# One chunk's second MLP in plain float32, its weight split moved to the next chunk's loads, and more masks on ScalarE

## The chip, the cores and the metric

The kernel runs on one core of a Trainium2 chip. The metric is the device time of one execution in microseconds (us), from launch to end; a lower time is better. The core has five engines that run their own instruction streams and wait for each other by semaphores: TensorE (PE; its weight loads are shown apart as PEld), VectorE (DVE), ScalarE (ACT), GpSimd (POOL) and SyncE (SP), which here only issues the DMAs.

## The reference

Three layers follow each other, all in float32: attention in which each query keeps its 32 best keys, and two MLPs over the 2304 rows (4 batches x 576 queries) of 512 features.

```python
scores = 0.125 * q @ k^T                  # 4 batches, 8 heads, 576 x 576, head size 64
kth    = 32nd largest of each row
attn   = softmax(where(scores >= kth, scores, -1e9));  x = attn @ v      # -> 2304 x 512
h = x @ w_in   (512 x 2048);   x = (h - tanh(h)) @ w_out                 # first MLP  (m = 0)
h = x @ w_in2  (512 x 2048);   x = where(h > 0, h, exp(min(h,0)) - 1) @ w_out2   # second MLP (m = 1)
```

## The kernel before, in words

The 2304 rows are cut into six chunks of 384 rows (`CHUNKS`; numbered 0 to 5 below, the "first chunk" is chunk 0). For each chunk the attention comes first and then the two MLPs; the MLPs of one chunk are woven into the attention of the next, so that TensorE has matmuls while VectorE looks for the 32 best keys.

**Attention.** A chunk has 4 head pairs and 8 groups of three 128-row tiles. A group takes four ticks of the hand-written order: in each tick `find` takes the eight largest of each tile (MAX8, L295) and, in the first three ticks, `drop` strikes them out (MATCH_REPLACE8, L309). In the fourth tick the rows are masked. VectorE does it with one instruction (L316), on exponentials that ScalarE made earlier (L299); or, for the first `MASK_ACT[chunk]` tiles of a group, ScalarE does it with a Prelu (L311) and an Exp that also sums (L312). `MASK_ACT` is 3 of 3 tiles in chunk 0, 1 of 3 in chunk 1, and 0 after that.

**MLPs.** An MLP has 16 steps (`ft`), 128 of the 2048 hidden features each. In a step `first` makes h from the 512 inputs (L435), ScalarE and VectorE apply the function (`gate`), and `second` adds the step's share to three PSUM banks (L471). Every product of float32 numbers is made from three products of "float32r" numbers: each operand is split into a rounded high part and a low rest (`split`, L114 to L116: ScalarE copies, GpSimd subtracts), and high x high, low weight x high and high weight x low are summed. So `first` has 12 matmuls of 384 columns a step and `second` 9 of 512 columns. The scores of chunk 0 (L270), attention x v (L355) and the small matmuls of the norm use plain float32, and the trace shows each of them as two instructions: L270 stands in the program 48 times and in the trace 96 times.

**Weights.** They come from outside as pairs of 32-bit words that are put together on the chip. `prepare` does this once for each of the 64 weight tiles of 128 x 512 (two MLPs, 16 steps, two halves), in chunk 0: a 512 KB load (`wr`), three ScalarE instructions (L144 to L146), one on VectorE (L147, `wf`), a GpSimd multiply (L150), then the split on ScalarE and GpSimd (`wp`, L152), and a store of high and low (512 KB) to a scratch in DRAM. Chunks 1 to 5 load high and low from it (L164, 512 KB). The eight pairs of tiles in `EARLY` (the first MLP's last four steps and the second MLP's first four) are prepared ahead, during chunk 0's attention, and chunk 0 loads them too. Weight tiles have 5 and 6 buffers, `wr` 3, `wf` 2; loads are issued 6 steps ahead.

**Order.** The order of the calls is written out by hand by ticks. From it a planner makes each engine's instruction order, by a simulated timeline, so an engine's order can differ from the program's where the plan sees a wait. All DMAs go through SyncE's queue in order. At the turn from the first to the second MLP, `between` copies the result (L485), transposes it (L488) and splits it into zh and zl (L490 on ScalarE, L491 on VectorE).

In the profile chunk 0's first MLP runs from about 188 to 286 us and its second from 290 to about 421 us, beside chunk 1's attention and the first groups of chunk 2's; chunk 1's second MLP and its weight loads, which are issued six steps earlier, follow between about 475 and 600 us. About the last 200 us hold chunk 5's MLPs alone.

Of the kernel before, what the change touches and what calls it, by code (L numbers as in the profile page):

```python
# [8 lines left out]
F32 = mybir.dt.float32  # L9
# [10 lines left out]
P = 128  # L20
# [25 lines left out]
MASK_ACT = [3, 1, 0, 0, 0, 0]  # L46
# [38 lines left out]
def tile_topk_attention_two_mlps(  # L85
# [35 lines left out]

    scratch = {
# [10 lines left out]
    def prepare(m, ft, half):  # L133

        raw = sb.tile([P, 512], I64, tag="wr", name=f"wr{m}_{ft}_{half}", bufs=RAW_BUFS)
        nc.sync.dma_start(raw, (w1, w2)[m][ft][:, half * 512 : half * 512 + 512])
        words = raw.bitcast(F32).rearrange("p (n w) -> p n w", w=2)  # L140
        sign = sb.tile([P, 512], BF16, tag="wsg", name=f"wsg{m}_{ft}_{half}", bufs=2)
        w = sb.tile([P, 512], F32, tag="wf", name=f"wf{m}_{ft}_{half}", bufs=2)
        low, scaled = words.bitcast(U32)[:, :, 0], words[:, :, 1]
        nc.scalar.activation(sign, words[:, :, 1], AF.Sign)  # L144
        nc.scalar.activation(scaled, words[:, :, 1], copy, scale=2.0**-112)  # L145
        nc.scalar.activation(low.bitcast(I32), low, copy, scale=2.0**-29 * (1 - 2.0**-20), bias=-0.5 + 7.5 * 2.0**-20)  # L146
        nc.vector.scalar_tensor_tensor(  # L147
            w.bitcast(U32), scaled.bitcast(U32), 3, low, op0=ALU.logical_shift_left, op1=ALU.bitwise_or
        )
        nc.gpsimd.tensor_mul(w, w, sign)  # L150
        wt = weight_tile(half, f"wp{m}_{ft}_{half}")
        split(wt[:, 0], wt[:, 1], w)  # L152
        nc.sync.dma_start(f(scratch[m, ft, half]), f(wt))
        return wt

    def load_next():
        if loads:
            ci, m, ft = loads.pop(0)
            for half in range(2):
                if ci == 0 and m * NF + ft not in EARLY:  # L160
                    weights[ci, m, ft, half] = prepare(m, ft, half)
                    continue
                wt = weights[ci, m, ft, half] = weight_tile(half, f"wt{ci}_{m}_{ft}_{half}")
                nc.sync.dma_start(f(wt), f(scratch[m, ft, half]))  # L164
# [261 lines left out]
    def first(ci, m, ft):  # L426
        n = SIZES[ci]
        xh, xl = x_tiles[ci] if m == 0 else z_tiles[ci]
        h = bank("h", f"h{ci}_{m}_{ft}", 2)[:, :n]
        wv = weights.pop((ci, m, ft, 0)).rearrange("p a (k c) -> p a k c", c=P)  # L430
        jobs = [(wi, xs, kt) for wi, xs in ((0, xh), (1, xh), (0, xl)) for kt in range(4)]
        late = (n // P - 1) * P
        for cs in (slice(0, late), slice(late, n)) if m == 1 and ft < PARTED and late else (slice(0, n),):
            for a, (wi, xs, kt) in enumerate(jobs):
                nc.tensor.matmul(h[:, cs], wv[:, wi, kt], xs[:, kt, cs], start=(a == 0), stop=(a == len(jobs) - 1))  # L435
# [8 lines left out]
    def gate(ci, m, ft):  # L444
        n = SIZES[ci]
        h, t = parts[ci, m, ft]
        g = sb.tile([P, NMAX], F32, tag="g", name=f"g{ci}_{m}_{ft}")[:, :n]
# [7 lines left out]
        gh = sb.tile([P, NMAX], F32R, tag="gh", name=f"gh{ci}_{m}_{ft}")[:, :n]  # L455
# [4 lines left out]
    def second(ci, m, ft):  # L460
# [5 lines left out]
        jobs = [(k, t) for k in range(3) for t in range(nt)]  # L466
        if ft == NF - 1:
            jobs.sort(key=lambda x: x[1])
        for k, t in jobs:
            gx, wi = ((gh, 0), (gh, 1), (gl, 0))[k]  # L470
            nc.tensor.matmul(  # L471
                acc[ci, m][:, t],
                gx[:, t * P : t * P + P],
                wt[:, wi],
                start=(ft == 0 and k == 0),
                stop=(ft == NF - 1 and k == 2),
            )

    def between(ci):

        a = acc.pop((ci, 0))
        z_tiles[ci] = zh, zl = tuple(sb.tile([P, NPAIR, NMAX], F32R, tag=f"x{c}", name=f"z{c}{ci}") for c in "hl")
        y = [sb.tile([P, 512], F32, tag="y", name=f"y{ci}_{t}", bufs=Y_BUFS) for t in range(SIZES[ci] // P)]
        for t in range(SIZES[ci] // P):
# [4 lines left out]
            cs = slice(t * P, t * P + P)  # L489
            nc.scalar.activation(zh[:, :, cs], pv, copy)  # L490
# [163 lines left out]
```

## Time and profile before

| | |
|---|---|
| time, median of 3 runs | 1289.49 us (1286.18 to 1289.66) |
| the profiled execution, its own time | 1289.64 us |
| its span, from the first to the last instruction | 1287.8 us |
| busy, share of the span: PE, PEld, DVE, ACT, POOL | 92%, 76%, 77%, 64%, 46% |
| granted TensorE clock, mean share of full speed | 0.963 |
| DMA, mean | 222 GB/s |

A busy PE is not a PE at its peak: matmuls overlap in the pipeline and their ends are modelled. For TensorE the spacing of matmuls in a long run says more than the mean duration of one. Idle time is charged to the last thing waited for.

### The profile page before, as it was taken

How to read it: one execution, taken by the hardware profiler on the slowest of the kernel's cores; microseconds unless marked ns; L12 is line 12 of the kernel's file. 1: busy time of each engine (PE TensorE's matmuls, PEld its weight loads, DVE VectorE, ACT ScalarE, POOL GpSimd, SP SyncE). 2: the span in 40 equal slices, each digit the busy share in tenths (PEclk: the TensorE clock that was granted, in tenths of full speed). 3: DMA queues.
4: the chain of work that ended last, by engine and by line, in shares of the span. 5: the costliest groups of instructions: out<-in, count | busy, mean ns of one | idle time of the engine just before them, and what ended most of it. 6: DMA issues, size and time to landing. Idle time of an engine off the chain costs nothing.

```text
span 1287.8 us, 19866 instructions
## 1 busy us (share of the span) xinstructions
PE 1189.0 (92%) x6424; PEld 981.9 (76%) x6424; DVE 993.4 (77%) x1950; ACT 819.2 (64%) x1780; POOL 592.4 (46%) x629
## 2 busy tenths in 40 slices
PE   4576889979989999999999999999999999999998
PEld 2333468758768888888877888988988978899896
DVE  7999999999899888789889789889888886100111
ACT  6999969898888445656556666566665545332333
POOL 4666559867886332434432344443334322233221
PEclk9976699989999999999999999999999999999999
DMA  7778446995778865667765668776677645677672
GB/s 249 241 254 263 152 145 225 326 285 170 243 234 316 286 218 167 213 221 251 222 204 178 208 226 270 234 222 197 222 214 235 208 150 182 210 252 257 215 246 76
DMA packets 97448, 286.14 MB, mean 222 GB/s; under 512 B 12096, under 2 KB 27968, under 8 KB 97344
## 3 DMA queue, kind: packets, MB, share of 16 engines
q1 hardware_dynamic: 97344, 284.87, 68.4%
q8 instruction: 51, 0.84, 0.3%
q14 instruction: 53, 0.43, 0.1%
HBM read 246.55 MB, written 38.27 MB: 221 GB/s over the span
## 4 chain that ended last, share of the span: by engine, by line
PE 68%; DVE 11%; ACT 10%; DMA 6%; issue 2%; POOL 2%; SPq 0%; POOLq 0%; ACTq 0%; DVEq 0%
PE h L435 28%; PE acc L471 26%; PE av L355 6%; DMA wr<-in_w_dram 5%; DVE vm L295 4%; PE pt L337 4%; DVE w L309 3%; PE ps L272 2%; PE ps L273 2%; DVE wf L147 2%; ACT wr L146 1%; ACT s L274 1%; ACT wr L145 1%; DMA kraw<-in_kT_dram 1%; ACT wp L115 1%
## 5 line engine op out<-in xcount | busy, mean ns | idle before, releaser
L116 POOL TENSOR_TENSOR gl<-g,gh 128x384 fp32r<-128x384 f32 x192 | 203.6, 1062 | 417.4 <-ACT gh L115 355.9
L295 DVE MAX8 vm<-w 128x8 f32<-128x576 f32 x432 | 321.0, 751 | 5.3
L471 PE MATMUL acc<-wt,gh 128*128 128x512 f32 x1008 | 271.6, 398 | 0.3 <-ACT gh L115 0.3
L309 DVE MATCH_REPLACE8 w<-vm,w 128x576 f32<-128x576 f32 x288 | 213.0, 740 | 0.0
L471 PEld LDWEIGHTS acc<-wt,gh 128*128 128x128 f32 x1008 | 184.7, 188 | 33.8 <-issue 1.2
L274 ACT ACTIVATE s<-ps 128x288 f32<-128x288 f32 (+1 forms) x320 | 125.5, 409 | 85.0 <-PE ps L273 78.8
L337 PE MATMUL pt<-ident,e 128*128 128x128 f32 (+1 forms) x720 | 120.1, 293 | 45.4 <-ACT e L312 25.9
L295 DVE MAX8 vm<-s 128x8 f32<-128x576 f32 x144 | 108.1, 750 | 64.9 <-ACT s L274 64.2
L435 PE MATMUL h<-zh,wt 128*128 128x384 f32 (+2 forms) x768 | 151.8, 329 | 5.5 <-ACT zh L490 3.9
L115 ACT ACTIVATE gh<-g 128x384 fp32r<-128x384 f32 x192 | 100.5, 525 | 87.5 <-DVE g L449 41.6
L471 PE MATMUL acc<-wt,gl 128*128 128x512 f32 x504 | 153.9, 401 | 0.8 <-POOL gl L116 0.8
L338 ACT ACTIVATE ph<-pt 128x384 f32<-128x384 f32 (+1 forms) x240 | 110.1, 490 | 53.5 <-PE pt L337 52.3
L337 PEld LDWEIGHTS pt<-ident,e 128*128 128x128 f32 (+1 forms) x720 | 89.8, 142 | 71.3 <-ACT e L312 28.7
L435 PE MATMUL h<-xh,wt 128*128 128x384 f32 x672 | 141.3, 340 | 1.6 <-DVE g L454 1.6
L435 PEld LDWEIGHTS h<-zh,wt 128*128 128x128 f32 x768 | 126.6, 193 | 17.0 <-ACT zh L490 5.3
L449 DVE SCALAR_TENSOR_TENSOR g<-t,h 128x384 f32<-128x384 f32 x96 | 52.2, 544 | 110.9 <-ACT t L441 110.6
L435 PEld LDWEIGHTS h<-xh,wt 128*128 128x128 f32 x672 | 117.4, 188 | 10.0 <-DVE g L454 1.8
L316 DVE SCALAR_TENSOR_TENSOR e<-s,vm,e 128x576 f32<-128x576 f32 x115 | 112.2, 981 | 2.6 <-ACT e L299 0.5
L471 PEld LDWEIGHTS acc<-wt,gl 128*128 128x128 f32 x504 | 92.3, 189 | 21.5 <-POOL gl L116 2.8
L355 PE MATMUL av<-ph,vraw 128*64 128x384 f32 (+3 forms) x640 | 106.1, 440 | 1.9 <-ACT s L274 1.9
L309 DVE MATCH_REPLACE8 w<-vm,s 128x576 f32<-128x576 f32 x144 | 106.6, 740 | 0.0
L116 POOL TENSOR_TENSOR wp<-wf,wp 128x512 fp32r<-128x512 f32 x64 | 87.5, 1368 | 29.8 <-ACT wp L115 29.1
(78 smaller groups left out, 2008.2 us busy)
## 6 DMA issues: line engine op xcount, KB each, us to landing
wt<-w SPq DMA_DIRECT2D x336, 512.0 KB, 4.3
wr<-in_w_dram SPq DMA_DIRECT2D x64, 512.0 KB, 4.7
w<-wp SPq DMA_DIRECT2D x64, 512.0 KB, 3.6
kraw<-in_kT_dram SPq DMA_DIRECT2D x120, 144.0 KB, 3.9
vraw<-in_vL_dram SPq DMA_DIRECT2D x64, 160.0 KB, 3.4
qraw<-in_qT_dram SPq DMA_DIRECT2D x88, 96.0 KB, 3.9
out_dram<-o SPq DMA_DIRECT2D x16, 256.0 KB, 6.3
out_dram<-o SPq DMA_DIRECT2D x4, 128.0 KB, 5.2
```

The source lines that it names most:

```text
L115: nc.scalar.activation(hi, src, copy)
L116: nc.gpsimd.tensor_sub(lo, src, f(hi))
L274: nc.scalar.activation(s[lo:hi, cs], pt[lo:hi, :HS], copy)
L295: nc.vector.max(g.vm[:, j, min(r, 1)], u.s[t] if r == 0 else g.w[j])
L309: nc.vector.match_replace(g.w[j], v, u.s[t] if r == 0 else g.w[j], FILL)
L316: nc.vector.scalar_tensor_tensor(u.e[t], u.s[t], v[:, 7:8], u.e[t], op0=ALU.is_ge, op1=ALU.mult, accum_out=g.sum[:, j : j + 1])
L337: nc.tensor.transpose(pt[:kn, j * P : j * P + P], v.e[t][:, k0 : k0 + kn], ident)
L338: nc.scalar.activation(g.ph[:kn, blk, :nq], pt[:kn, :nq], copy)
L355: nc.tensor.matmul(pt[h * D : h * D + D, :n], v.vraw[h][:kn, blk], v.g.ph[:kn, blk, cs], start=(blk == 0), stop=(blk == NB - 1),)
L435: nc.tensor.matmul(h[:, cs], wv[:, wi, kt], xs[:, kt, cs], start=(a == 0), stop=(a == len(jobs) - 1))
L449: nc.vector.scalar_tensor_tensor(g, t, -1.0, h, op0=ALU.add, op1=ALU.max)
L471: nc.tensor.matmul(acc[ci, m][:, t], gx[:, t * P : t * P + P], wt[:, wi], start=(ft == 0 and k == 0), stop=(ft == NF - 1 and k == 2),)
```

## The change

The second MLP of chunk 0, and only that one, takes plain float32 operands: one product instead of three, so 4 matmuls in `first` and 3 in `second` for each step in the program. Its weights are then not split in `prepare`: GpSimd's multiply writes the weight tile itself, and 256 KB go to a scratch of their own (`single`). zl, the split of the gate and gl are left out for it. When chunk 1 loads these 32 tiles it loads 256 KB, splits them (ScalarE and GpSimd) and stores the 512 KB that chunks 2 to 5 load. `MASK_ACT` of chunk 1 goes from 1 to 3. The diff, without the lines that only rename:

```diff
-MASK_ACT = [3, 1, 0, 0, 0, 0]
+MASK_ACT = [3, 3, 0, 0, 0, 0]
...
-        nc.gpsimd.tensor_mul(w, w, sign)
         wt = weight_tile(half, f"wp{m}_{ft}_{half}")
-        split(wt[:, 0], wt[:, 1], w)
-        nc.sync.dma_start(f(scratch[m, ft, half]), f(wt))
+        if m == 1:
+            nc.gpsimd.tensor_mul(f(wt[:, 0]), w, sign)
+            nc.sync.dma_start(single[m, ft, half], f(wt[:, 0]))
+        else:
+            nc.gpsimd.tensor_mul(w, w, sign)
+            split(wt[:, 0], wt[:, 1], w)
+            nc.sync.dma_start(f(scratch[m, ft, half]), f(wt))
...
+            if ci == 0 and m == 1:
+                nc.sync.dma_start(f(wt[:, 0]), single[m, ft, half])
+            elif ci == 1 and m == 1:
+                nc.sync.dma_start(f(wt[:, 1]), single[m, ft, half])
+                split(wt[:, 0], wt[:, 1], f(wt[:, 1]))
+                nc.sync.dma_start(f(scratch[m, ft, half]), f(wt))
+            else:
                 nc.sync.dma_start(f(wt), f(scratch[m, ft, half]))
...
+        plain = (ci, m) == (0, 1)
+        if plain:
+            jobs = [(f(wv[:, 0, kt]), f(xs[0][:, kt])) for kt in range(4)]
...
+        if (ci, m) == (0, 1):
+            parts[ci, m, ft] = gh, None
+            return
...
+        terms = ((f(gh), f(wt[:, 0])),) if (ci, m) == (0, 1) else ((gh, wt[:, 0]), (gh, wt[:, 1]), (gl, wt[:, 0]))
...
+            if ci == 0:
+                nc.scalar.activation(f(zh[:, :, cs]), pv, copy)
+                continue
             nc.scalar.activation(zh[:, :, cs], pv, copy)
             nc.vector.tensor_sub(zl[:, :, cs], pv, f(zh[:, :, cs]))
```

## Rows read from the trace of the kernel before

**Rows 1.** Busy time by engine in stretches (length; busy us; clock; DMA share, GB/s).

```profile
154.00:174.00 20.00, 17.02 (x79) 10.30 (x78) 18.11 (x39) 14.80 (x35) 6.78 (x11) 0.91 0.23 62
174.00:194.00 20.00, 17.56 (x87) 15.66 (x86) 20.00 (x42) 13.58 (x29) 15.21 (x14) 0.91 0.56 191
194.00:217.00 23.00, 21.83 (x123) 19.91 (x122) 23.00 (x43) 21.30 (x46) 22.57 (x25) 1.00 0.74 243
217.00:241.00 24.00, 22.91 (x151) 18.51 (x150) 23.93 (x45) 22.32 (x49) 22.40 (x22) 1.00 0.81 262
241.00:262.00 21.00, 19.32 (x111) 17.37 (x110) 20.73 (x44) 16.75 (x37) 13.51 (x16) 1.00 1.02 356
262.00:281.00 19.00, 14.73 (x107) 10.37 (x105) 19.00 (x36) 17.51 (x40) 15.18 (x16) 1.00 1.01 294
290.00:421.00 131.00, 122.28 (x720) 102.31 (x721) 124.86 (x240) 111.41 (x243) 100.09 (x92) 0.97 0.72 242
505.00:600.00 95.00, 95.00 (x520) 81.36 (x519) 81.06 (x163) 56.85 (x127) 35.50 (x39) 1.00 0.71 224
```

**Rows 2.** The chain that ended last, single pieces (start us, length us, what).

```profile
82.52 1.98 ACT e L311 x3
...
199.14 0.77 DVE e L316 x2
...
272.01 9.04 DMA kraw<-in_kT_dram
...
283.14 5.09 DMA wr<-in_w_dram
...
323.19 4.33 DMA wr<-in_w_dram
...
801.59 3.70 PE av L355 x40
...
1140.82 2.10 PE acc L471 x9
1142.92 2.08 PE h L435 x12
```

**Rows 3.** Instruction groups of the whole run (count; busy us, mean ns).

```profile
L116 POOL TENSOR_TENSOR gl<-g,gh 128x384 fp32r<-128x384 f32 x192 | 203.6, 1062 | 417.4 <-ACT gh L115 355.9 <-PE acc L471 38.2 <-PE ps L273 12.8
...
L316 DVE SCALAR_TENSOR_TENSOR e<-s,vm,e 128x576 f32<-128x576 f32 x115 | 112.2, 981 | 2.6 <-ACT e L299 0.5
...
L115 ACT ACTIVATE gh<-g 128x384 fp32r<-128x384 f32 x192 | 100.5, 525 | 87.5 <-DVE g L449 41.6 <-PE acc L471 16.2 <-DVE g L454 15.7
...
L116 POOL TENSOR_TENSOR wp<-wf,wp 128x512 fp32r<-128x512 f32 x64 | 87.5, 1368 | 29.8 <-ACT wp L115 29.1
...
L115 ACT ACTIVATE wp<-wf 128x512 fp32r<-128x512 f32 x64 | 40.6, 634 | 4.1 <-POOL wf L150 4.1
...
L312 ACT ACTIVATION_READ_ACCUMULATOR e<-e,b 128x1 f32 x29 | 6.0, 206 | 0.0
```

**Rows 4.** TensorE on line L435 in one stretch (matmuls, then weight loads).

```profile
290.00:421.00 131.00, 52.89 (x276) 46.76 (x276) 0.97 0.72 242
```

**Rows 5.** The same for line L471, in two stretches.

```profile
290.00:421.00 131.00, 41.60 (x153) 27.20 (x154) 0.97 0.72 242
505.00:600.00 95.00, 42.81 (x162) 29.60 (x162) 1.00 0.71 224
```

**Rows 6.** TensorE's timeline at 73 us (start, length of the run, what).

```profile
73.16 0.89 PE L270 MATMUL ps<-kraw,qraw 64*128 64x288 f32 x3
```

**Rows 7.** Line L270 (count; ns min/median/max, first and last start).

```profile
L270 PE MATMUL ps<-kraw,qraw x96: 402/685/847, 4.3 to 141.0; 64*128 64x288 f32 x96
```

**Rows 8.** DMA issues from 505 to 600 us (count, size, median us to landing).

```profile
wt<-w SPq DMA_DIRECT2D x34, 512.0 KB, 4.3
```

**Rows 9.** The same from 225 to 290 us.

```profile
wt<-w SPq DMA_DIRECT2D x16, 512.0 KB, 8.4
```

**Rows 10.** SyncE's waits over the whole run (us in total, times, longest).

```profile
SPq L139 <- DVE wf L147: 68.1, 40, 4.0
```

More of the change, by code (lines that the diff above doesn't have):

```diff
@@ L119, in bank @@
         return ps.tile([P, 512], F32, tag=tag, name=name, bufs=bufs)
+    single = {
+        (m, ft, half): dr.tile([P, 512], F32, tag=f"f{m}_{ft}_{half}", name=f"f{m}_{ft}_{half}")
+        for m in range(1, 2)
+        for ft in range(NF)
+        for half in range(2)
+    }
     scratch = {
@@ L149, in prepare @@
         )
-        nc.gpsimd.tensor_mul(w, w, sign)
         wt = weight_tile(half, f"wp{m}_{ft}_{half}")
-        split(wt[:, 0], wt[:, 1], w)
-        nc.sync.dma_start(f(scratch[m, ft, half]), f(wt))
+        if m == 1:
[5 more added lines that the diff above has]
+            nc.sync.dma_start(f(scratch[m, ft, half]), f(wt))
         return wt
     def load_next():
[L157 to L163, printed above, removed]
+        if not loads:
+            return
+        ci, m, ft = loads.pop(0)
+        for half in range(2):
+            if ci == 0 and m * NF + ft not in EARLY:
+                weights[ci, m, ft, half] = prepare(m, ft, half)
+                continue
+            wt = weights[ci, m, ft, half] = weight_tile(half, f"wt{ci}_{m}_{ft}_{half}")
+            if ci == 0 and m == 1:
[5 more added lines that the diff above has]
+            else:
                 nc.sync.dma_start(f(wt), f(scratch[m, ft, half]))
@@ L427, in first @@
         n = SIZES[ci]
-        xh, xl = x_tiles[ci] if m == 0 else z_tiles[ci]
+        xs = x_tiles[ci] if m == 0 else z_tiles[ci]
+        plain = (ci, m) == (0, 1)
         h = bank("h", f"h{ci}_{m}_{ft}", 2)[:, :n]
         wv = weights.pop((ci, m, ft, 0)).rearrange("p a (k c) -> p a k c", c=P)
-        jobs = [(wi, xs, kt) for wi, xs in ((0, xh), (1, xh), (0, xl)) for kt in range(4)]
+        if plain:
+            jobs = [(f(wv[:, 0, kt]), f(xs[0][:, kt])) for kt in range(4)]
+        else:
+            jobs = [(wv[:, wi, kt], x[:, kt]) for wi, x in ((0, xs[0]), (1, xs[0]), (0, xs[1])) for kt in range(4)]
         late = (n // P - 1) * P
         for cs in (slice(0, late), slice(late, n)) if m == 1 and ft < PARTED and late else (slice(0, n),):
-            for a, (wi, xs, kt) in enumerate(jobs):
-                nc.tensor.matmul(h[:, cs], wv[:, wi, kt], xs[:, kt, cs], start=(a == 0), stop=(a == len(jobs) - 1))
+            for a, (w, x) in enumerate(jobs):
+                nc.tensor.matmul(h[:, cs], w, x[:, cs], start=(a == 0), stop=(a == len(jobs) - 1))
         t = sb.tile([P, NMAX], F32, tag="t", name=f"t{ci}_{m}_{ft}")[:, :n]
@@ L465, in second @@
         gh, gl = parts.pop((ci, m, ft))
-        jobs = [(k, t) for k in range(3) for t in range(nt)]
+        terms = ((f(gh), f(wt[:, 0])),) if (ci, m) == (0, 1) else ((gh, wt[:, 0]), (gh, wt[:, 1]), (gl, wt[:, 0]))
+        jobs = [(k, t) for k in range(len(terms)) for t in range(nt)]
         if ft == NF - 1:
@@ L469, in second @@
         for k, t in jobs:
-            gx, wi = ((gh, 0), (gh, 1), (gl, 0))[k]
+            gx, w = terms[k]
             nc.tensor.matmul(
@@ L473, in second @@
                 gx[:, t * P : t * P + P],
-                wt[:, wi],
+                w,
                 start=(ft == 0 and k == 0),
-                stop=(ft == NF - 1 and k == 2),
+                stop=(ft == NF - 1 and k == len(terms) - 1),
             )
```

9 lines of the change are left out of this document (6 added, 3 removed).

## The prediction

> **What bounds the kernel now.** I read the busy time by stretches first, cut at the groups of chunk 1's attention [rows 1]. Up to 281 us VectorE is full (from 174 us on it idles 0.3 us in a stretch at most) while TensorE still has gaps. From 505 to 600 us it is the other way round: TensorE 95.00 of 95, VectorE 81.06. So what is saved on VectorE counts only before about 421 us, and whatever TensorE is given costs time as soon as its gaps are used up. ScalarE must be read beside VectorE: in 194 to 217, 217 to 241 and 262 to 281 us it idles only 1.70, 1.68 and 1.49 us; in the other three stretches 4.25 to 6.4 us.
>
> Then the chain of waits [rows 2]. Between 270 and 380 us it runs through the making of weights: DMAs of `wr` (5.09 and 4.33 us shown, two of some eight), each issued when VectorE's L147 has freed a raw buffer (SyncE waited 68.1 us for L147 in all [rows 10]), and one `kraw` DMA of 9.04 us at 272 us, where the 16 DMA engines were full (share 1.02 and 1.01 [rows 1]). Late in the run the chain is only `first` and `second`: 2.08 us for 12 matmuls, 2.10 us for 9 [rows 2], so a step costs TensorE 4.18 us.
>
> **Masks: 16 leave VectorE.** Chunk 1 has 8 groups, and two more tiles of each go to ScalarE. On VectorE each takes 0.77 us at best (the chain's piece with its sum read) and 0.98 us by the mean, 1.06 with the read [rows 2, 3]. On ScalarE each adds a Prelu at 0.66 us (three in 1.98 us [rows 2]) and a sum read of 0.1 to 0.21 us [rows 3]; the Exp was there before and only moves to the fourth tick. A group thus sheds 1.5 to 2.1 us of VectorE and gains 1.5 to 1.7 us of ScalarE. Six groups lie in the six stretches before 281 us. In three of them ScalarE's idle time is just what is added, so VectorE's gain is lost to ScalarE; in the other three it counts: 3 x 1.5 to 2.1 = 4.6 to 6.4 us. ScalarE's own waits for others don't all vanish, so I take **-4.0** (bounds 0 and -12.7, which is six full groups). Behind the later Exp the group's transposes wait; they come in the next tick or the one after, some 5 us on, and are covered while TensorE has step work.
>
> **Shorter making of weights, less traffic at the turn.** Of the 32 tiles of the second MLP 8 are prepared early, 24 in the stage. Each sheds a ScalarE copy (634 ns) and a GpSimd subtract (1368 ns) [rows 3], and 256 KB of store; the 8 early ones also come back as 256 KB. At the turn, around 241 to 281 us, those are 8 x 256 KB = 2.1 MB less in full DMA queues, at 294 to 356 GB/s some 6 us of transfer. Loads there landed after 8.4 us [rows 9], elsewhere 4.3 [rows 8], and behind the 5.09 us DMA at 283 us stands the ScalarE work on `wr`, with zh of the turn behind it. VectorE was full until 281 us, so only part reaches the end: **-1.5** (0 to -4.1, the difference of the two landings). The planner makes new orders here, so this is the softest term.
>
> **The second MLP of chunk 0, 290 to 421 us.** It sheds 16 gate splits on ScalarE (525 ns) and GpSimd (1062 ns) [rows 3], 24 weight splits as above, three zl on VectorE and the last four masks. ScalarE loses 16 x 0.525 + 24 x 0.634 = 23.6 us less 4 x 0.8, GpSimd 16 x 1.06 + 24 x 1.37 = 50 us: both fall far from full, and VectorE has at least 3 us more. TensorE becomes the question. A plain float32 matmul is two instructions; one of 128 rows by 128 columns of weights isn't in the trace, L270's 64 by 128 is nearest. Three of L270 at full clock took 0.89 us, the last of them 0.40 [rows 6, 7], so they start (0.89 - 0.40)/2 = 0.245 us apart for 288 columns, hence 0.326 for 384 and 0.435 for 512. `first` takes 8 x 0.326 = 2.61, `second` 6 x 0.435 = 2.61: 5.22 us a step in place of 4.18, +1.04. The first two steps are cut in 256 and 128 columns, where 12 + 12 float32r matmuls have no such advantage; I count nothing for their `first` and half for their `second`: 14 x 1.04 + 2 x 0.5 = **+15.6 us of TensorE's time**. Bounds: what those three rows leave, 0.245 to 0.297 (0.89/3), the upper one being +34 us; I stay at the lower, for the run's last matmul must end before it can be counted.
>
> Does it fit? In 290 to 421 us TensorE issues 720 matmuls [rows 1]: 276 of L435 and 153 of L471 [rows 4, 5]. L435 is 19 whole `first` and 2 cut ones (48 pieces, 2.7 us each `first`): 19 x 2.08 + 5.4 = 44.9; L471 17 x 2.10 = 35.7. The other 291 belong to attention. In 505 to 600 us the full TensorE ran 18 steps (162/9 [rows 5]) = 75.2 us, and the rest of 95 us went to attention: 155 others or a little more, 0.128 us each. At that price 291 cost 37.2, so the stretch holds 118 us of work, of 131; with the change 133, 2 us over. But 80 of the 291 are half-width attention x v, 40 in 3.70 us [rows 2], 0.0925 each: 2.8 us less, 130.6. So TensorE's gaps are just used up: between -3 and +4 I take **-0.5**. Here the change's VectorE gain is worth nothing.
>
> **A rule against it.** The row gives plain float32 a price of 5.22/4.18 = 1.25 of the split form. The Trainium skill, FP8 and Floating Point Precision, section TensorE Precision Notes, says that true float32 takes four passes through the array; against three products of one pass that would be a third more, 16 x 4.18/3 = 22.3 us in place of 15.6, by estimate, and the sum would be some 6.7 us worse. The trace agrees with the four (two instructions, each at half the column rate), but here a float32r matmul also costs more than its columns, which the rule leaves out; the row decides.
>
> **Chunk 1's second MLP, about 475 to 600 us.** It gains 32 loads of 256 KB in place of 512, 32 splits and 32 stores of 512 KB. ScalarE gets 32 x 0.634 = 20.3 us, GpSimd 32 x 1.368 = 43.8: over 95 us they go from 56.9 to 77 and from 35.5 to 79 [rows 1]. DMA gains 8.4 MB, 88 GB/s: 224 becomes 312, near the 294 to 356 at which loads landed after 8.4 us. Behind a split on ScalarE that waits for its load stand the copies of scores, the gate's exponentials and gh; behind a store in SyncE's queue that waits for GpSimd stand the next weights and `kraw`. Weights have five steps, some 25 us, to be ready, so TensorE need not starve. In 194 to 241 us ScalarE was at 93% and GpSimd at 96%, and TensorE 44.7 of 47 busy, 95% where it was 100% here; with engines at 80% I take a third of those five points of 95 us: **+1.5** (0 to +15, next part).
>
> **Sum.** -4.0 - 1.5 - 0.5 + 1.5 = -4.5 us against the profiled execution's 1289.64 (span 1287.8 and 1.8 around it; 0.15 above the median of the runs, which is nothing): **1285**.
>
> **Rivals.** 0.3% (3.9 us) is about what can be told from no change: faster is below 1285.6, slower above 1293.4.
>
> (a) Forecast, 1282 to 1288, chance 0.40, a little over half of it below 1285.6.
>
> (b) ScalarE copes, and VectorE's whole 12.7 us before 281 us count, with TensorE's gaps used fully (-3) and no loss later: 1272 to 1281. For it: VectorE is the full engine in every one of those stretches. Against: ScalarE's idle 1.5 to 1.7 us in three. Chance 0.20.
>
> (c) No change, 1288 to 1293: TensorE takes all back in 290 to 421 us (+4 for its term), as by the rule of four passes (the skill's page above; by it 1291 to 1292), or the turn falls no better. For it: TensorE's gaps there are 13 us against 15.6 added. Chance 0.20, a fifth of it over 1293.4.
>
> (d) Slower, 1294 to 1305: ScalarE blocks in chunk 1's loads. Its queue is in order and placed by a plan; if a split stands before its load has landed, ScalarE stands too. It has 95 - 77 = 18 us to give; 32 splits each held over 0.56 us use that up, and from there TensorE waits. Held 1.0 to 1.5 us (loads land 4.1 us later under such traffic) they cost 14 to 30 us against 6 gained: +8 and more. A dear plain float32 (the +34) would also end there. Against: five steps of lead. Chance 0.20.
>
> Faster 0.46, same 0.30, slower 0.24. The range is **1275 to 1298**: it leaves out the far ends of (b) and (d), and (a) alone is 1282 to 1288.
>
> **What will show it.** In the changed profile: L471 and L435 in chunk 0's second MLP as 6 and 8 instructions a step at 0.43 and 0.33 us; TensorE without gaps there; ScalarE full in 194 to 281 us; the end of chunk 0's second MLP (421 us before) some 6 us earlier; GpSimd near 80% and DMA above 300 GB/s in chunk 1's second MLP, TensorE still full. I am wrong if that end does not move (c), if it moves 12 us or more (b), or if chunk 1's part is longer by more than 5 us with ScalarE waiting for `wt` DMAs (d).

## The result and the profile after

The changed kernel took 1297.04 us (median of 6 runs, 1292.43 to 1299.26) where the kernel before took 1288.65 (6 runs, 1285.70 to 1290.98): ratio 1.0064, 95% interval 1.0042 to 1.0085. That is 8.3 us slower, where 4.5 us faster was forecast. Below, a ratio is turned into us by 1289.5, so that all kernels can be set side by side; an interval of 0.0036 is 4.6 us wide.

First the page of each kernel: busy time of the engines over the whole span, before and then after.

```profile
span 1287.8 us, 19866 instructions
PE 1189.0 (92%) x6424; PEld 981.9 (76%) x6424; DVE 993.4 (77%) x1950; ACT 819.2 (64%) x1780; POOL 592.4 (46%) x629
```

```profile
span 1294.6 us, 19645 instructions
PE 1200.3 (93%) x6304; PEld 961.2 (74%) x6304; DVE 971.6 (75%) x1915; ACT 826.6 (64%) x1796; POOL 569.6 (44%) x613
```

The span is TensorE's busy time and TensorE's idle time. Busy rose by 11.3 us, idle fell from 98.8 to 94.3, which together is the 6.8 us between the two profiled spans. VectorE and GpSimd both lost over 20 us of work, and the time grew all the same.

Busy time by stretches of the changed kernel (columns as in [rows 1]: length; busy us of PE, PEld, DVE, ACT, POOL, each with its count; clock; DMA share, GB/s). The first five stand against the same stretches there; the next three end where chunk 0's second MLP, chunk 1's first and chunk 1's second end, by the copy of the last output tile.

```profile
174.00:194.00 20.00, 18.29 (x98) 15.63 (x98) 19.97 (x36) 18.44 (x40) 16.69 (x17) 1.00 0.60 208
194.00:217.00 23.00, 21.94 (x119) 19.64 (x118) 21.52 (x43) 22.51 (x50) 19.87 (x21) 1.00 0.69 235
217.00:241.00 24.00, 22.68 (x153) 18.55 (x152) 19.66 (x34) 22.00 (x47) 18.64 (x21) 1.00 1.01 356
241.00:262.00 21.00, 18.40 (x103) 15.87 (x101) 16.60 (x33) 18.82 (x44) 10.79 (x11) 1.00 0.86 267
262.00:281.00 19.00, 16.10 (x116) 12.24 (x115) 18.98 (x38) 18.14 (x43) 9.32 (x14) 0.91 0.45 141
257.80:408.40 150.60, 135.12 (x598) 81.78 (x599) 115.12 (x222) 108.83 (x237) 54.53 (x65) 0.94 0.55 179
408.40:497.40 89.00, 87.04 (x486) 73.73 (x484) 83.38 (x172) 55.30 (x124) 45.64 (x47) 1.00 0.73 240
497.40:601.90 104.50, 102.03 (x566) 86.83 (x565) 89.39 (x177) 72.25 (x160) 66.68 (x62) 0.98 0.78 264
505.00:600.00 95.00, 94.82 (x527) 80.12 (x526) 80.13 (x156) 65.48 (x147) 62.32 (x58) 1.00 0.78 265
```

The same three milestones of the kernel before, which have no row ahead of the prediction:

```profile
274.00:416.10 142.10, 127.26 (x752) 105.03 (x749) 135.32 (x260) 123.70 (x270) 109.34 (x106) 0.95 0.72 241
416.10:490.70 74.60, 73.91 (x393) 63.19 (x392) 63.13 (x126) 35.78 (x81) 24.83 (x28) 1.00 0.77 248
490.70:592.20 101.50, 99.73 (x561) 86.14 (x560) 86.77 (x176) 61.44 (x136) 34.63 (x38) 0.98 0.64 203
```

Read the two together. Chunk 0's first MLP ended 16.2 us earlier (257.8 against 274.0), its second 7.7 us earlier: up to there the kernel looks faster. Then chunk 1's first MLP lasts 89.0 us in place of 74.6, at a full TensorE in both, and the lead is a lag of 6.7 us. `second` has 144 matmuls in it in both kernels and `first` 173 against 150; the other matmuls, nearly all of them attention's, are 169 against 99. So most of the 87.04 against 73.91 us of TensorE is attention that had not been done by 408 us. VectorE's searches (MAX8) show the same: at 408.4 us the changed kernel has started 222 of them and the kernel before 233, and by the end of chunk 1's first MLP both have 274. So the end of an MLP says little here about progress: attention was left behind and paid where TensorE has no gap.

The chain of waits in that stretch is now almost all TensorE (start us, length us, what):

```profile
376.43 2.58 PE acc L497 x6
379.00 2.58 PE h L457 x8
...
401.62 2.09 PE h L457 x12
```

A plain float32 step is 2.58 + 2.58 = 5.16 us (5.22 had been worked out), beside 4.18 for the split form [rows 2]; chunk 1's `first` in the last line still is 2.09. The DMAs that chunk 1 was feared to suffer from, by issue, 505 to 600 us (count, size, median us to landing), and below them who waits for what from 408 to 602 us (us in total, times, longest):

```profile
w<-wt SPq DMA_DIRECT2D x21, 512.0 KB, 4.0
wt<-w SPq DMA_DIRECT2D x13, 512.0 KB, 4.3
wt<-f SPq DMA_DIRECT2D x21, 256.0 KB, 3.6
```

```profile
POOL gl L116 <- ACT gh L115: 47.7, 19, 4.4
POOL wt L116 <- ACT wt L115: 15.2, 15, 3.1
ACT wt L115 <- DMA wt<-f: 13.3, 14, 2.3
...
PE ps L290 <- DVE zl L521: 1.3, 1, 1.3
PE h L457 <- ACT zh L520: 1.0, 1, 1.0
```

The queues are not full (265 GB/s; the loads of 512 KB land as in [rows 8]), and TensorE waits a few us in all. ScalarE does stand before the late split for its load, 13.3 us. SyncE's wait for the making of weights did not shrink: it was 68.1 us [rows 10] and is 75.7 us now (42 times, the longest 5.4 us).

### The profile page after: what moved, and what is told of

It reads as the page before. It is cut to its first block, busy times and chain, and to the rows that moved or that the text cites. A ratio compares the mean times of both kernels' runs of the same rounds, so it can differ in the third digit from the quotient of the medians.

```text
span 1294.6 us, 19645 instructions
## 1 busy us (share of the span) xinstructions
PE 1200.3 (93%) x6304; PEld 961.2 (74%) x6304; DVE 971.6 (75%) x1915; ACT 826.6 (64%) x1796; POOL 569.6 (44%) x613
## 4 chain that ended last, share of the span: by engine, by line
PE 67%; ACT 13%; DMA 7%; DVE 7%; issue 3%; POOL 2%; SPq 0%; POOLq 0%; ACTq 0%; DVEq 0%
PE h L457 27%; PE acc L497 26%; DMA wr<-in_w_dram 5%; PE av L373 5%; PE pt L355 4%; DVE vm L313 3%; PE ps L290 2%; DVE w L327 2%; PE ps L291 2%; ACT wr L152 1%; ACT e L330 1%; DVE wf L153 1%; ACT wsg L150 1%; ACT s L292 1%; ACT wr L151 1%
## 5 line engine op out<-in xcount | busy, mean ns | idle before, releaser
L116 POOL TENSOR_TENSOR gl<-g,gh 128x384 fp32r<-128x384 f32 x176 | 186.7, 1061 | 384.6 <-ACT gh L115 342.2
L497 PE MATMUL acc<-wt,gh 128*128 128x512 f32 x1008 | 281.7, 406 | 3.7 <-DVE gh L472 2.6
L457 PE MATMUL h<-zh,wt 128*128 128x384 f32 (+2 forms) x768 | 155.5, 335 | 5.8 <-ACT zh L520 5.1
L497 PE MATMUL acc<-wt,gl 128*128 128x512 f32 x492 | 149.2, 399 | 0.8 <-POOL gl L116 0.8
L457 PE MATMUL h<-xh,wt 128*128 128x384 f32 x672 | 143.9, 340 | 0.0
L115 ACT ACTIVATE gh<-g 128x384 fp32r<-128x384 f32 x176 | 92.0, 523 | 69.5 <-DVE g L472 35.2
L472 DVE SCALAR_TENSOR_TENSOR g<-t,h 128x384 f32<-128x384 f32 x80 | 43.7, 546 | 112.9 <-ACT t L463 110.0
L462 ACT ACTIVATE t<-h 128x384 f32<-128x384 f32 x96 | 46.6, 486 | 87.4 <-PE h L457 87.1
L477 DVE TENSOR_TENSOR g<-h,t 128x384 f32<-128x384 f32 x76 | 41.5, 548 | 72.4 <-ACT t L460 71.4
```

The costliest lines, as they stand in the source:

```text
L115: nc.scalar.activation(hi, src, copy)
L116: nc.gpsimd.tensor_sub(lo, src, f(hi))
L457: nc.tensor.matmul(h[:, cs], w, x[:, cs], start=(a == 0), stop=(a == len(jobs) - 1))
L462: nc.scalar.activation(t, h, AF.Relu, scale=-1.0)
L472: nc.vector.scalar_tensor_tensor(g, t, -1.0, h, op0=ALU.add, op1=ALU.max)
L497: nc.tensor.matmul(acc[ci, m][:, t], gx[:, t * P : t * P + P], w, start=(ft == 0 and k == 0), stop=(ft == NF - 1 and k == len(terms) - 1),)
```

## The experiments

All medians are over several runs, and each ratio is against the kernel before on the same chip. e3, e4, e6, e7 and e14 to e17 leave out or replace work that the result needs; they only put a price on a part.

| run | edit | us | ratio, 95% interval | us against before |
|---|---|---|---|---|
| e6_lighter_alone | lighter chunk 0 alone | 1278.36 | 0.9901 (0.9879 to 0.9923) | -12.8 |
| e5_plain_alone | plain float32 alone | 1300.61 | 1.0067 (1.0048 to 1.0086) | +8.6 |
| e3_three_products | change without plain float32 | 1287.98 | 0.9983 (0.9967 to 0.9998) | -2.2 |
| e4_no_late_split | change without late split | 1292.16 | 1.0015 (1.0001 to 1.0029) | +1.9 |
| e7_split_no_store | late split, no store | 1299.62 | 1.0063 (1.0048 to 1.0078) | +8.1 |
| e16_split_scalar_only | its ScalarE part alone | 1297.77 | 1.0059 (1.0039 to 1.0079) | +7.6 |
| e17_split_gpsimd_only | its GpSimd part alone | 1292.94 | 1.0022 (1.0008 to 1.0036) | +2.8 |
| e9_split_a_step_later | split one load step later | 1295.43 | 1.0041 (1.0026 to 1.0057) | +5.3 |
| e11_no_masks_split_later | the same, masks as before | 1297.27 | 1.0045 (1.0028 to 1.0062) | +5.8 |
| e18_split_on_gpsimd | split all on GpSimd, masks as before | 1310.72 | 1.0149 (1.0132 to 1.0166) | +19.2 |
| e8_multiply_in_place | weight made in place, ScalarE copies | 1308.87 | 1.0131 (1.0111 to 1.0151) | +16.9 |
| e2_no_masks | change without the masks | 1295.66 | 1.0043 (1.0027 to 1.0059) | +5.5 |
| e1_masks_alone | masks alone, 3 of 3 | 1296.06 | 1.0051 (1.0032 to 1.0069) | +6.6 |
| e13_two_masks | 2 of 3 | 1292.28 | 1.0015 (1.0003 to 1.0028) | +1.9 |
| e12_masks_all_on_dve | 0 of 3 | 1291.58 | 1.0021 (1.0006 to 1.0036) | +2.7 |
| e10_masks_rounding_on_dve | masks alone, a rounding moved | 1297.47 | 1.0051 (1.0036 to 1.0066) | +6.6 |
| e14_no_masks_relief | 1 of 3, the others not masked | 1287.08 | 0.9973 (0.9960 to 0.9986) | -3.5 |
| e15_late_exponential | the same, exponential late | 1284.93 | 0.9958 (0.9945 to 0.9970) | -5.4 |

**The lighter chunk 0.** The changed kernel with the masks as before, the float32r product of the high parts three times in place of plain float32, and no late split:

```diff
-MASK_ACT = [3, 3, 0, 0, 0, 0]
+MASK_ACT = [3, 1, 0, 0, 0, 0]
...
-            jobs = [(f(wv[:, 0, kt]), f(xs[0][:, kt])) for kt in range(4)]
+            jobs = [(wv[:, 0, kt], xs[0][:, kt]) for _ in range(3) for kt in range(4)]
...
+        terms = ((gh, wt[:, 0]),) * 3 if (ci, m) == (0, 1) else ((gh, wt[:, 0]), (gh, wt[:, 1]), (gl, wt[:, 0]))
...
+            elif m == 1:
+                nc.sync.dma_start(f(wt), single[m, ft, half].unsqueeze(1).to_broadcast([P, 2, 512]))
```

> The changed kernel without all three suspects: three float32r products of the same operands, no late split (both halves loaded from the 256 KB scratch), masks of chunk 1 as before. What is left is the lighter preparation, gate and turn of chunk 0. Its output is not the MLP's. If the parts add up (price of plain float32 about 10, late split 6, masks 3 of a loss of 8), it is 10 to 13 us faster than before: 1277 to 1280 us. If they overlap, and only one of them can be saved at a time, it is within 4 us of the kernel with three products, 1284 to 1288 us.

1278.36 us, 12.8 less than before: this is by far the largest effect of any part, and it had been put at 1.5. Its page:

```profile
span 1273.4 us, 19765 instructions
PE 1181.3 (93%) x6424; PEld 980.4 (77%) x6424; DVE 976.5 (77%) x1947; ACT 798.5 (63%) x1732; POOL 530.1 (42%) x581
```

TensorE's idle time fell from 98.8 to 92.1 us, its busy time by 7.7 at the same number of matmuls. The mean granted clock of the two profiles is 0.968 of full speed against 0.963, and that alone is some 6 us of 1181 (an estimate); why it is higher was not tried.

VectorE is busy 16.9 us less with only three instructions fewer. Two kinds became shorter, the making of weights and the masks: L147 before, then the same two lines in e6 (L316 before is in [rows 3], with 981 ns).

```profile
L147 DVE SCALAR_TENSOR_TENSOR wf<-wr 128x512 uint32<-128x512 uint32 x64 | 59.3, 927 | 4.5 <-ACT wr L145 2.5 <-POOL wp L116 1.2 <-POOL kk L116 0.5
```

```profile
L332 DVE SCALAR_TENSOR_TENSOR e<-s,vm,e 128x576 f32<-128x576 f32 x115 | 102.9, 901 | 2.3 <-ACT e L315 0.3
L153 DVE SCALAR_TENSOR_TENSOR wf<-wr 128x512 uint32<-128x512 uint32 x64 | 54.1, 845 | 6.1 <-issue 4.3 <-POOL wp L116 0.7 <-ACT wr L151 0.4
```

In the trace before, each of the 32 masks and 22 L147 that took over 1000 ns ran beside GpSimd instructions for more than a fifth of its time. Those that ran so took 1147 and 998 ns in the mean, the others 807 and 675. So less work on GpSimd also shortens work on VectorE. e6 takes 20.7 us of work off ScalarE and 62.3 off GpSimd at once, and stores with them; which of them gives the 12.8 us was not tried.

**Plain float32.** First alone in the kernel before, as shown here, then taken out of the changed kernel (the edit of e6 without its lines on the masks and the late split).

```diff
+        plain = (ci, m) == (0, 1)
+        g32 = f if plain else (lambda ap: ap)
+        jobs = [(wi, xs, kt) for wi, xs in ((0, xh), (1, xh), (0, xl))[: 1 if plain else 3] for kt in range(4)]
...
+                nc.tensor.matmul(h[:, cs], g32(wv[:, wi, kt]), g32(xs[:, kt, cs]), start=(a == 0), stop=(a == len(jobs) - 1))
```

> The kernel before, with one change: in chunk 0's second MLP the high x high product is taken in plain float32 and the two others are left out (so the low parts are split as before but not used; the output is a little less exact). This adds TensorE's price alone. By the runs so far (the changed kernel against the one with three products: 9 to 10 us) it is 8 to 12 us slower than before, 1297 to 1301 us. By the prediction's sum (TensorE's gaps take it) it is at most 3 us slower.

> The changed kernel, but chunk 0's second MLP takes three float32r products of the same (rounded) operands in place of one plain float32 product: 12 and 9 matmuls a step as before, so TensorE's price is the old one and everything else is as changed. Its output is not the MLP's. If the price of plain float32 (5.16 us a step against 4.18) is the loss, this saves some 14 us: 1281 to 1285 us. If the waits in the making of weights are the loss (GpSimd's multiply now waits for a weight buffer), TensorE's saving only becomes more waiting: over 1291 us.

It costs 8.6 us alone and 8.3 + 2.2 = 10.5 us in the changed kernel. The pages of the two, plain float32 alone first:

```profile
span 1298.8 us, 19621 instructions
PE 1200.6 (92%) x6304; PEld 963.8 (74%) x6304; DVE 996.6 (77%) x1950; ACT 821.5 (63%) x1780; POOL 588.3 (45%) x629
```

```profile
span 1283.6 us, 19884 instructions
PE 1184.3 (92%) x6424; PEld 980.6 (76%) x6424; DVE 966.8 (75%) x1915; ACT 826.3 (64%) x1796; POOL 570.2 (44%) x613
```

Alone, TensorE's busy time rises by 11.6 us over before and its idle time is 98.2, against 98.8: in these profiles nothing was absorbed. In the changed kernel busy is 16.0 us more than with three products, and idle 94.3 against 99.3: a third was absorbed. In the second MLP of chunk 0 itself, with three products:

```profile
258.40:398.20 139.80, 122.79 (x738) 104.62 (x739) 119.40 (x236) 112.29 (x245) 57.10 (x67) 0.93 0.60 196
```

TensorE idles 17.0 us there, and 15.5 in the row of the changed kernel (135.12 of 150.60) with 12.3 us more work in it. The gaps are still there when the work is added, and the stretch is 10.8 us longer.

**The late split.** Without it, the single goes to both halves of the tile (e4). With its two operations but no store (e7), and with the one or the other operation alone. The edits stand here in one, and the comments name the runs that have a line:

```diff
-                nc.sync.dma_start(f(wt[:, 1]), single[m, ft, half])
-                split(wt[:, 0], wt[:, 1], f(wt[:, 1]))
-                nc.sync.dma_start(f(scratch[m, ft, half]), f(wt))
+                nc.sync.dma_start(f(wt), single[m, ft, half].unsqueeze(1).to_broadcast([P, 2, 512]))
+                if ci == 1:                                                   # e7, e16, e17
+                    split(wt[:, 0], wt[:, 1], f(wt[:, 1]))                    # e7
+                    nc.scalar.activation(wt[:, 0], f(wt[:, 1]), copy)         # e16
+                    nc.gpsimd.tensor_sub(wt[:, 1], f(wt[:, 1]), f(wt[:, 0]))  # e17
```

> The changed kernel without the late split: chunks 1 to 5 load each of the second MLP's weight tiles from the 256 KB scratch into both halves of the tile (512 KB in one DMA); no split, no second store in chunk 1. It leaves out the rounding into high and low, so its output is not the MLP's. If the 32 splits and stores in chunk 1 disturb TensorE, this saves 3 to 10 us against the changed kernel; if they are hidden, it stays within 2 us of it.

> The changed kernel with the late split's work on ScalarE and GpSimd kept, but loads of 512 KB as before (from the 256 KB scratch, twice) and no store; chunks 2 to 5 load the same way. The output is not the MLP's, since the later chunks have no split weights. If ScalarE and GpSimd (and their waits for the loads) are what the late split costs, it equals the changed kernel, 1294 to 1299 us. If the 512 KB stores are, it equals the kernel without the late split, 1290 to 1294 us.

> The changed kernel with 512 KB loads and no late store, and of the late split ScalarE's rounding copy alone: GpSimd's subtraction is left out, so the low parts of the second chunk's second MLP are not the low parts. With both engines' work it took 1299.6 us, with neither 1292.2. If ScalarE's copy, which waits for the load at the head of an in-order queue, is the cost, 1297 to 1300; if GpSimd's subtraction is, 1291 to 1294.

> The same with GpSimd's subtraction alone: ScalarE's rounding copy is left out, so the low parts are zero. If ScalarE's copy is the cost, 1291 to 1294; if GpSimd's subtraction is (it shares what VectorE needs, or holds GpSimd's queue), 1297 to 1300. Half each, 1295 to 1297 in both runs, if the two engines' work simply adds up.

The late split costs 8.3 - 1.9 = 6.4 us, the stores nothing that shows (e7 is level with the changed kernel). ScalarE's copy alone costs 7.6 - 1.9 = 5.7 us, GpSimd's subtraction alone 0.9, whose intervals with e4 overlap. GpSimd's instruction is the longer one; ScalarE's is the dear one. In the run with ScalarE's part alone, 408 to 602 us:

```profile
ACT wt L180 <- DMA wt<-f: 15.6, 17, 2.7
```

Is it that wait, or the copy's own time? The split was issued one load step after its load:

```diff
+        while waiting:
+            wt, to = waiting.pop(0)
+            split(wt[:, 0], wt[:, 1], f(wt[:, 1]))
+            nc.sync.dma_start(f(to), f(wt))
...
-                split(wt[:, 0], wt[:, 1], f(wt[:, 1]))
-                nc.sync.dma_start(f(scratch[m, ft, half]), f(wt))
+                waiting.append((wt, scratch[m, ft, half]))
```

> The changed kernel, but each late split stands one load step behind its load in the program, so that the load has landed when ScalarE comes to it. In the changed kernel ScalarE waited 13.3 us (14 times) for these loads between 408 and 602 us. If that wait is what the late split costs, this is 4 to 7 us faster than the changed kernel, 1290 to 1293 us. If the 32 copies and subtracts themselves are the cost, it stays within 2 us of it.

> The changed kernel without the masks and with the late split one load step behind its load: the version that the runs point to if waits for loads cost the 6 us. By the parts (plain float32 +9, lighter chunk 0 -13, late split 0 to +6) 1285 to 1292 us; as fast as before if the split is free there, 1294 to 1297 us if it is not.

5.3 and 5.8 us over before: the first is 3.0 us better than the changed kernel, but the intervals overlap, and with the masks as before the later split gains nothing (5.8 us against the 5.5 of e2, which has the split in its old place). Nor did the edit take the wait away: from 408 to 602 us ScalarE still waited 11.2 us in 13 times for these loads in e9, and 18.3 in 19 in e11, against 18.7 in 19 in e2. So what the wait alone costs was not settled. Then both of ScalarE's new loads were taken away: masks as before, and GpSimd rounds as well.

```diff
-                split(wt[:, 0], wt[:, 1], f(wt[:, 1]))
+                nc.gpsimd.tensor_copy(wt[:, 0], f(wt[:, 1]))
+                nc.gpsimd.tensor_sub(wt[:, 1], f(wt[:, 1]), f(wt[:, 0]))
```

> The changed kernel with one mask of three (as before) on ScalarE for the second chunk, and with GpSimd making the late split whole: it rounds the loaded single and subtracts, and ScalarE does nothing for it. ScalarE's copy was worth 4.9 us (1297.8 with it alone, 1292.9 with GpSimd's subtraction alone) and the masks 2.7 us in the changed kernel. If ScalarE's time is the price of both, the time is 1288 to 1291 us, level with before; if GpSimd's added copy holds the loads as long, or slows VectorE, 1294 to 1298, no better than the changed kernel.

A miss: 19.2 us slower than before. Instruction groups on GpSimd from 408 to 620 us (busy us, mean ns, then the idle time ahead and what ended it):

```profile
L180 POOL TENSOR_TENSOR wt<-wt 128x512 fp32r<-128x512 f32 x32 | 42.2, 1321 | 0.3
L116 POOL TENSOR_TENSOR gl<-g,gh 128x384 fp32r<-128x384 f32 x32 | 33.6, 1052 | 26.3 <-ACT gh L115 23.1 <-PE acc L498 3.0
L179 POOL CAST wt<-wt 128x512 fp32r<-128x512 f32 x32 | 20.5, 643 | 15.5 <-DMA wt<-f 14.2 <-PE pt L356 0.6 <-issue 0.4
```

The rounding takes GpSimd 643 ns, no more than ScalarE, but the wait for the load has moved to GpSimd (14.2 us in 5 times, the longest 6.3), and behind it stand `gl` and GpSimd's add ahead of the reciprocals of the sums, which TensorE's steps and the attention need. Chunk 1's second MLP became 126.9 us long, TensorE busy in 115.1 of them (104.5 and 102.0 in the changed kernel); the profiled execution was the fastest of the five, 1302.79 us. That this wait is the reason was read from these rows, not tried.

**The weight buffer.** In the changed kernel GpSimd's multiply writes the weight tile itself, and so waits 14.7 us for `second` to free it. Here it multiplies in place, and ScalarE copies:

```diff
-            nc.gpsimd.tensor_mul(f(wt[:, 0]), w, sign)
-            nc.sync.dma_start(single[m, ft, half], f(wt[:, 0]))
+            nc.gpsimd.tensor_mul(w, w, sign)
+            nc.scalar.activation(f(wt[:, 0]), w, copy)
+            nc.sync.dma_start(single[m, ft, half], w)
```

> The changed kernel, but GpSimd multiplies in place as before, and ScalarE copies the product into the weight tile (24 more copies of 0.63 us in chunk 0, and 8 early ones); the 256 KB store reads the product. So the wait for a free weight buffer stands on ScalarE again and no longer in GpSimd's queue (23 us of GpSimd waiting for TensorE from 270 to 425 us in the changed kernel). If that wait holds chunk 0's second MLP back, this is 3 to 8 us faster than the changed kernel. If it only stands where GpSimd had nothing to do, it is the same or slower by the copies: 1295 to 1302 us.

16.9 us over before, 8.6 over the changed kernel. So freeing GpSimd from that wait gains less than 32 more copies on ScalarE cost; the two were not tried apart.

**The masks.** In the changed kernel without them, alone, with none of three, and with two of three (the comment names the runs):

```diff
-MASK_ACT = [3, 3, 0, 0, 0, 0]
+MASK_ACT = [3, 1, 0, 0, 0, 0]    # e2; from the kernel before: [3, 3, ...] e1, [3, 0, ...] e12, [3, 2, ...] e13
```

> The changed kernel with chunk 1's masks back on VectorE (1 of 3 on ScalarE). If the masks gave a part of the 16.2 us and it lasts, this kernel is slower than the changed one by 3 to 10 us (1300 to 1307 us). If VectorE's relief is worth nothing once TensorE is the bound, it equals the changed kernel within 3 us.

> The kernel before with ScalarE's masks of chunk 1 alone. In the changed kernel chunk 0's first MLP ended 16.2 us earlier (last copy at 257.8 us against 274.0). If the masks did that, this kernel ends its first MLP near 260 us too, and, with no plain float32 behind it, keeps some 8 to 14 us to the end: 1275 to 1281 us. If the early end came from the lighter weights instead, or ScalarE is too full for the masks, the time stays within 4 us of the kernel before.

> The kernel before with chunk 1's masks all on VectorE (0 of 3 on ScalarE). If a mask costs more on ScalarE than on VectorE at the end of the run (16 more there cost 6.6 us), 8 fewer give some 3 us: 1285 to 1288 us. If VectorE's work decides, as the prediction had it, 8 masks of 0.77 to 1.06 us come back on it: 1294 to 1298 us.

> The kernel before with two of three masks of the second chunk on ScalarE in place of one. Zero of three was 2.7 us slower than one, three of three 6.6 us slower. If the loss grows with ScalarE's extra work in proportion, the time is 1292 to 1294 us; if the first mask handed over is still a gain and only the third spoils it, 1286 to 1290.

In the changed kernel the masks cost 8.3 - 5.5 = 2.8 us, at overlapping intervals. Alone they cost 6.6, where 4.0 were to be gained; from none to three the times against before are +2.7, 0, +1.9 and +6.6 us. The old setting is the best, and the loss grows with each mask from there. Was ScalarE merely too full in chunk 0's first MLP? Then giving VectorE a rounding in exchange should help:

```diff
+        if (ci, m) == (0, 0):
+            nc.vector.tensor_copy(gh, g)
+            nc.gpsimd.tensor_sub(gl, g, f(gh))
+        else:
+            split(gh, gl, g)
```

> The kernel before with ScalarE's masks of chunk 1, and in exchange VectorE rounds the gate's result of chunk 0's first MLP (16 copies of 128 x 384 that ScalarE did at 0.52 us). If masks alone lost because ScalarE was the full engine from 193 to 268 us (94, 90 and 92% busy there, VectorE 90, 82 and 81%), this takes 4 to 7 us of that back: 1289 to 1293 us. If they lost because the Exp comes a tick later and the transposes wait for it, it stays at 1295 to 1298 us.

It did not: 1.0051 again, the time that had been expected if the transposes wait for the later Exp. So the masks' two effects were tried one by one, VectorE's relief first, then with the exponential where ScalarE's mask has it, but no Prelu ahead:

```diff
                 # e14: exponential at its old place gives the sum, no mask on VectorE
+                kw = {"accum_out": g.sum[:, j : j + 1]} if u.ci == 1 else {}
+                nc.scalar.activation(u.e[t], u.s[t], AF.Exp, bias=g.mb[:, j : j + 1], scale=SCALE, **kw)
...
-            else:
+            elif u.ci != 1:
...
                 # e15: exponential in the fourth tick, no mask on VectorE
-            if r == 1 and j >= by_act:
+            if r == 1 and j >= by_act and u.ci != 1:
...
+            elif u.ci == 1:
+                nc.scalar.activation(
+                    u.e[t], u.s[t], AF.Exp, bias=g.mb[:, j : j + 1], scale=SCALE, accum_out=g.sum[:, j : j + 1]
+                )
```

> The kernel before without the second chunk's VectorE masks: for the two tiles of three that VectorE masked, the mask is left out and the exponential, at its old place, gives the sum itself, so attention there runs over all keys. VectorE is relieved as in the kernel with all masks on ScalarE and ScalarE gets nothing more. If ScalarE's extra work is what the masks lose, this gains what the relief of VectorE is worth, 2 to 6 us: 1283 to 1288. If a VectorE that runs ahead is itself what costs (its work finished earlier moves attention into the part where TensorE is full), it loses like the masks: 1294 to 1297.

> As the run without the second chunk's VectorE masks (the mask left out again, attention over all keys in those tiles), but the exponential is issued where ScalarE's own mask has it, two turns later, without the Prelu ahead of it. If the Prelu's time on ScalarE is the loss, this stays with the run before it, 1283 to 1288. If the place of the exponential is the loss (it comes just before the transposes that read it, and ahead of the gate's exponentials in ScalarE's queue), it is slower by most of the 6.6 us: 1292 to 1296.

The relief of VectorE is worth 3.5 us, and 5.4 with the exponential late; the intervals of the two overlap. From there to the masks alone lie 5.4 + 6.6 = 12.0 us, of which the two intervals leave some 3 either way. Sixteen Prelus are added, but not they alone. ScalarE's own mask needs the threshold, which GpSimd makes (`nk`) when the fourth search of all three tiles is done; e15's exponential needs only the row's largest value, which is known from the first tick. In the masks' run the Prelus (ns min/median/max, first and last start us), and then, from the groups of 148 to 425 us, busy time and the idle time ahead of the Prelu:

```profile
L311 ACT ACTIVATE e<-s,nk x45: 758/770/789, 35.0 to 340.8; 128x576 f32<-128x576 f32 x45
```

```profile
L311 ACT ACTIVATE e<-s,nk 128x576 f32<-128x576 f32 x24 | 16.8, 767 | 1.0 <-POOL nk L301 0.9
```

Before, there are 29 Prelus, so 16 more. By their mean they take 16 x 0.767 = 12.3 us, but neighbours on ScalarE overlap at their ends: between the two pages its busy time differs by 9.5 us. The pages, masks alone first, then with the exponential late:

```profile
span 1295.6 us, 19853 instructions
PE 1192.0 (92%) x6424; PEld 984.5 (76%) x6424; DVE 977.4 (75%) x1918; ACT 831.5 (64%) x1812; POOL 589.4 (45%) x629
```

```profile
span 1284.6 us, 19821 instructions
PE 1187.6 (92%) x6424; PEld 982.1 (76%) x6424; DVE 976.1 (76%) x1918; ACT 822.0 (64%) x1796; POOL 587.8 (46%) x629
```

VectorE is the same in both. TensorE idles 103.6 us with the Prelus and 97.0 without, and is busy 4.4 us longer for the same number of matmuls (mean granted clock 0.961 against 0.965). When the masks of chunk 1's last group are ready differs by far more than the Prelus' time: in the masks' run first, then in e15 (start us, length us, what):

```profile
339.49 2.10 ACT L311 ACTIVATE e<-s,nk 128x576 f32<-128x576 f32 x3
...
343.11 0.77 ACT L312 ACTIVATE e<-e,b 128x576 f32<-128x576 f32 x1
```

```profile
323.59 0.76 ACT L316 ACTIVATE e<-s,mb 128x576 f32<-128x576 f32 x1
...
325.11 0.77 ACT L312 ACTIVATE e<-e,b 128x576 f32<-128x576 f32 x1
```

The group's last exponential ends at 347.8 us in the masks' run and at 325.9 in e15, and in all eight groups it is 10 to 23 us earlier in e15, though by 350 us VectorE has started 200 and 201 searches in the two. So the 12.0 us are the price of ScalarE's way of masking as a whole; how much of it is the Prelus' time, and how much the wait for the threshold and the later transposes, was not tried apart. How a ScalarE that idles an eighth of that stretch can hold TensorE shows in the timeline of the masks alone:

```profile
346.26 0.77 ACT L312 ACTIVATE e<-e,b 128x576 f32<-128x576 f32 x1
...
346.69 0.29 PE L273 MATMUL ps<-kk,qs 128*128 128x288 f32 x1
...
347.02 0.77 ACT L312 ACTIVATE e<-e,b 128x576 f32<-128x576 f32 x1
347.68 0.20 ACT L312 ACTIVATION_READ_ACCUMULATOR e<-e,b 128x1 f32 x1
347.77 0.52 ACT L441 ACTIVATE t<-t 128x384 f32<-128x384 f32 x1
...
348.54 0.51 DVE L449 SCALAR_TENSOR_TENSOR g<-t,h 128x384 f32<-128x384 f32 x1
...
349.11 2.29 PE L435 MATMUL h<-zh,wp 128*128 128x384 f32 x6 [2.13 <-DVE g L449]
```

The gate's exponential (L441) stands in ScalarE's queue behind the exponentials of two masks (their Prelus had run at 339.49 us); VectorE's gate follows it, and TensorE's next `first`, which needs the bank that the gate frees, stands idle for 2.13 us. This is one such place, read from the trace; the sum over all of them was not made. Why the exchange in e10 brought nothing stays open.

No run here that computes what the reference does was faster than the kernel before.

## Why the prediction was wrong

The parts as measured: lighter chunk 0 -12.8, plain float32 +10.5, late split +6.4, masks +2.8 in the changed kernel, in sum +6.9 against the +8.3 of the whole, whose interval reaches from 5.4 to 11.0. The forecast had -1.5, -0.5, +1.5 and -4.0. Point by point:

**Plain float32: the step that failed is "So TensorE's gaps are just used up".** The price itself was right: 5.16 us a step against 5.22, and 16.0 us of busy time in the changed kernel against 15.6, though only 11.6 alone. (The upper bound, +34, is 32 by the prediction's own count of steps; nothing hangs on it.) The rule weighed against it, four passes (the Trainium skill, FP8 and Floating Point Precision, section TensorE Precision Notes), would have asked for 22.3 by estimate; the row decided rightly. But the 13 us of gaps were counted as room, and in the changed kernel TensorE still idles 15.5 us in that stretch, against 17.0 with three products. By the traces these gaps are waits in a chain that runs through ScalarE, VectorE and TensorE in turn, which longer matmuls lengthen; that was read, not tried. Of the added busy time two thirds (10.5 of 16.0 us) to three quarters (8.6 of 11.6) came through by the medians, and nearly all in the two profiled spans of plain float32 alone and before (11.0 of 11.6).

**Masks: the step that failed is the price of ScalarE's share.** VectorE's relief, forecast as a gain of 4.0, is a gain of 3.5 to 5.4 by the runs without the mask, but the match is luck: the 4.0 are what was left after half the groups had been given up to a full ScalarE, and with nothing to do on ScalarE the six groups were good for up to 12.7. The work added on ScalarE was set against its idle time, group by group, as a loss of gain at worst ("in the other three it counts"). Its way of masking cost 12.0 us, for 9.5 us more of ScalarE's busy time. The whole, +6.6 alone, lies outside the bounds given (0 to -12.7): as with TensorE, idle time was taken for room. The later transposes were put at nothing as "covered"; the exponentials that they read come 10 to 23 us later than in e15, so this term may have failed too, and that stays open.

**Shorter making of weights and the lighter second MLP of chunk 0: mis-sized.** Forecast -1.5 with bounds 0 to -4.1; it measured -12.8. The term that was missed is the work taken off ScalarE (some 24 us of copies) and GpSimd (50 us) [rows 3] in chunk 0's second MLP: both were said to "fall far from full", and this was priced at nothing beyond the turn. Nor did the sum have that VectorE's own instructions become shorter beside a GpSimd with less to do. Which of these gives the gain stays open.

**Late split: right mechanism in part, wrong size.** +1.5 was taken of 0 to +15, and it cost 6.4. Rival (d) named ScalarE, and ScalarE's copy is what costs. But its point of decision was not reached: ScalarE stood 13.3 us before loads, 0.4 us a split and not 0.56, and was busy 72.25 of 104.5 us. DMA above 300 GB/s and loads at 8 us did not come (265 GB/s, 3.6 us), and chunk 1's second MLP is 3.0 us longer (104.5 against 101.5), under the 5 that were to tell (d). In the profile the cost does not show as waits of TensorE in that stretch, and where the time is lost was not found.

**Milestone: right and useless.** The end of chunk 0's second MLP was to come some 6 us earlier and came 7.7 earlier. The prediction would have taken that as a sign for its forecast; the attention left behind took it back by 497 us.

So the time is that of rival (d) (1294 to 1305), and the late split on ScalarE, which (d) named, is a part of it. That the sum landed there is luck: plain float32 cost more (10.5) at the price per step that the forecast gave it, the masks lost where they were to gain, and the lighter chunk 0 gave 12.8 back.

## What to carry to other kernels

An engine's idle time is room only if work can be put into it without moving what another engine waits for: where a chain passes through several engines in order, work added to any of them, ScalarE at 84% (148 to 425 us before) or TensorE at 90%, can come through in large part or more than whole (10.5 of 16.0 us for plain float32, 12.0 for 9.5 us of ScalarE's masks). Price an edit first by the engine time that it adds on such a path, and only then subtract what a named cover hides. And where work is ordered by a planner over several stages, compare TensorE's busy and idle time over the whole span, not the end of one stage, which can come earlier because something else was left undone.

## What the runs showed of the hardware

- A plain float32 matmul with 128x128 weights takes two instructions; in long runs they stand 0.43 us apart for 512 columns (2.58/6) and 0.32 for 384 (2.58/8), in all 1.23 times the three float32r products.
- A rounding of 128x512 float32 takes GpSimd 643 ns as a cast (ScalarE 632 to 634), its subtraction of the same size 1321 ns.
- VectorE instructions that read two tiles in SBUF get longer beside GpSimd: in the kernel before, L316 takes 807 ns and L147 675 in the mean where GpSimd works beside them for less than a fifth of their time, 1147 and 998 where for more. L449 and L454, which read one operand from PSUM, do not: 545 and 551 ns without, 541 and 542 beside it.
